# First pair of chunks: invert 16x16 blocks only and finish by block substitution on TensorE

## The chip, the cores and the metric

The kernel runs on one core of a Trainium2 chip. The metric is the device time of one execution in microseconds; the time before is the median of three runs, and one more execution was profiled. The engines are called as in the profile: PE is TensorE, PEld its weight loads, DVE is VectorE, ACT is ScalarE, POOL is GpSimd, SP is SyncE, which issues most DMAs.

## What is computed

Three layers follow each other; the change lies in the first.

```python
# 1: delta-rule attention, 32 heads (4 x 8), 768 steps, head size 48
k_n = k / (norm(k) + 1e-6)
for t in range(768):
    y[t] = q[t] @ state
    v_old = state.T @ k_n[t]
    state += beta[t] * outer(k_n[t], v[t] - v_old)
# 2: soft mixture of 8 experts, weights P from 8 Sinkhorn rounds over x @ w_gate
out = sum_e P[:, e] * (relu(x @ w1[e]) @ w2[e])
# 3: ((x @ w1) * (x @ w2)) @ w3 @ w_out
```

The 768 steps are cut into 12 chunks of 64. Inside a chunk the steps are solved together: with G the Gram matrix of the chunk's keys, L its strict lower triangle with rows scaled by beta, a chunk needs u = inverse(I + L) times (scaled v minus what the old state predicts). From u follow the chunk's output and the new state.

## The kernel before, in words

**Layout.** A chunk holds 32 heads x 64 steps: 128 partitions are two groups of 64 steps, and 16 heads lie side by side in each. Two chunks make a pair (j = 0 to 5). A "quad group" below is the helper `quads`: 32 small matmuls in float32, four at a time in the four 64x64 tiles of the array. The trace shows each float32 matmul as two records, so a quad group is 64 records.

**A pair's preparation.** `prep_k` loads keys, squares and sums them (ACT, DVE), takes Sqrt on ACT and a Newton step on DVE (`newton`), computes the Gram matrices (PE, "b<-kt") and copies them out of PSUM into `a` and `g`. `invert` then inverts all the 32x32 diagonal blocks of a pair together on DVE: a transposition, 7 small product-and-sum steps for 8x8 blocks, products of 512 elements for 16x16 blocks, products of 1024 elements for 32x32 blocks, and two transpositions (L602, L604). `tt_make` joins two 32x32 inverses to a 64x64 one by PE matmuls of 32x32 ("b<-asys,g" and "b<-tt,g") and copies; the result is `tt`. `prep_q` computes the masked products of queries and keys (`pt`).

**A chunk's recurrence.** `seq(c)`: the old state predicts v ("b<-st,kt"), DVE subtracts, PE multiplies by the inverse ("b<-vs,tt"), two ACT copies give `u`, "b<-u,kraw" the state (copied to `st` on ACT) and "b<-pt,u" the output. The output is copied to `xst` (ACT), goes to DRAM and comes back in another layout (the DMAs xs_d<-xst and xst<-xs_d), and is split by ACT and POOL or DVE into the high and low part `xr`.

**The first expert beside it.** `e0(c)` computes expert 0 for the 256 tokens of a chunk: 144 matmuls with 128x128 weights and 256 columns ("b<-xr,wA" and "b<-hA,wA"). It needs the chunk's `xr` and has the lowest priority, so PE fills its gaps with it. The router's logits are "b<-xr,wg" and "b<-masks,yr". After chunk 11 come the Sinkhorn rounds ("b<-cs,ones"), then the other experts and the third layer.

**What sets the order.** Everything is recorded as operations with priorities; a planner in the program (`Plan.order`) places them by its own cost figures and writes each engine's list before anything runs. On the chip each engine follows its list in order, and waits at the head of it.

Two columns of the small input `masks` (64 and 65) hold -1 for the first and for the second 32 steps of 64; with them ACT and DVE copy the two 32x32 diagonal blocks of a Gram matrix into `a`.

Of the kernel before, what the change touches and what calls it, by code (L numbers as in the profile page):

```python
# [6 lines left out]
F32 = mybir.dt.float32  # L7
# [11 lines left out]
NG = 16  # L19
D = 48  # L20
# [290 lines left out]
def act(n, psum=False):  # L311
    return (n / 1.2 + (110 if psum else 150)) / 1000
# [22 lines left out]
class Kernel:  # L335
# [56 lines left out]
    def setup(self):  # L392
        nc, T, g = self.nc, self.T, self.g
        n = NCH * NG
        self.open("const", "left", ones=((128, 128), F32), masks=((128, 75), F32),
                  wgr=((128, 3, NE), F32), p=((128, NTT + 1, NE + 1), F32),
# [24 lines left out]
        self.bank = [pp.tile([128, 512], F32, tag=f"b{i}", name=f"b{i}") for i in range(8)]  # L421
        self.psum = Ring(range(8), caps={"attn": 4, "eh": 1, "ey": 1, "hx": 6, "yb": 2, "h": 4, "y": 4})
        a = self.a
# [35 lines left out]
    def prep_k(self, c):  # L459
# [8 lines left out]
        sq = lambda: T["kn"][:, kn.at]  # L468
        g.op({"ACT": act(768)}, lambda e: nc.scalar.activation(out=sq(), in_=sq(), func=AF.Square), r=[], w=[kn], prio=pr)
        nr = lambda i: T["nrm"][:, i]  # L470
        g.op({"DVE": dve(768) + .07}, lambda e: nc.vector.tensor_reduce(out=nr(0)[:, 16 * st:16 * st + 16], in_=sq(), axis=AX.X, op=ALU.add),  # L471
             r=[kn], w=[("n0", st)], prio=pr)
        if st:
            n0 = [("n0", 0), ("n0", 1)]
            bm = lambda: T["bm"][:, 32 * j:32 * j + 32]
            nv = lambda: T["nv"][:, 32 * j:32 * j + 32]
            g.op({"DVE": .1}, lambda e: nc.vector.tensor_scalar(out=nr(0), in0=nr(0), scalar1=1e-30, scalar2=None, op0=ALU.max), w=n0, prio=pr)
            g.op({"ACT": .15}, lambda e: nc.scalar.activation(out=nr(1), in_=nr(0), func=AF.Sqrt), r=n0, w=["n1"], prio=pr)
# [10 lines left out]
            g.op({"DVE": 1.3}, newton, r=n0 + ["bm"], w=["n1", ("bm", j), ("nv", j)], prio=pr)  # L489
        gi = j % NG12  # L490
        pg = pr if j == 0 else -120.0 + j
# [7 lines left out]
        g.op({"PE": 8 * QUAD}, gram, ins=128, r=[k], w=sg + [(self.a0[j], "z")] + [  # L499
            (n, gi, st, hf) for n in ("g12", "xsb0", "xsb1") for hf in range(2)], prio=pg)  # L500
        for hf in range(2):
            gs = slice(8 * hf, 8 * hf + 8)
            s = sg[hf]
            ss = slice(16 * st + 8 * hf, 16 * st + 8 * hf + 8)
            a0 = self.a0[j]
            ak = (a0, st, hf)
            g.op({"ACT": act(256, True)}, lambda e, s=s, ss=ss, a0=a0: self.copy(
                "ACT", T["a0"][:, a0.at, ss], self.ps(s, 8, 64)[:, :, 0:32], T["masks"][:, 64:65]), r=[s, "masks"], w=[ak], prio=pg)
            g.op({"ACT": act(256, True)}, lambda e, s=s, gs=gs, st=st: self.copy(
                "ACT", T["g12"][:, gi, st, gs], self.ps(s, 8, 64)[:, :, 32:64], -1.0),  # L510
                r=[s], w=[(n, gi, st, hf) for n in ("g12", "xsb0", "xsb1")], prio=pg)
            g.op({"DVE": dve(256)}, lambda e, s=s, ss=ss, a0=a0: self.stt(
                T["a0"][:, a0.at, ss], self.ps(s, 8, 64)[:, :, 32:64], T["masks"][:, 65:66], T["a0"][:, a0.at, ss], ALU.mult, ALU.add),
                r=[s, "masks", ("g12", gi, st, hf)], w=[ak], prio=pg)

# [15 lines left out]
    def invert(self, j):  # L531
# [75 lines left out]
    def tt_make(self, c):  # L607

        nc, g, T = self.nc, self.g, self.T
        st = c % 2  # L610
        pr = 10.0 * (c // 2) + 2 + st
        a0 = self.a0[c // 2]
        gi = c // 2 % NG12
        tt = self.TT[c] = self.ttring.new()
        bk = ("bm", c // 2)
        for hf in range(2):
            gs = slice(8 * hf, 8 * hf + 8)
# [36 lines left out]
            for b in range(2):  # L654
# [3 lines left out]
                    r=[s2, bk], w=[tk(1 + b)], prio=pr)  # L658

    def prep_q(self, c):  # L660

        nc, g, T = self.nc, self.g, self.T
        pr = 10.0 * (c // 2) + 2.5 + c % 2
        pd = pr if c > 1 else 4.0
        q = self.Q[c] = self.qring.new()
        self.dma(lambda: T["qt"][:, q.at].rearrange("p g t -> p (g t)"), lambda: self.a["qT"][c], 524288, [], [q], pr - 20)
        k = self.K[c]
        sp = [self.psum.new("attn") for _ in range(2)]
        for hf in range(2):
# [6 lines left out]
        for hf in range(2):  # L676
            s, pt = sp[hf], self.PT[c, hf]
            g.op({"DVE": dve(512)}, lambda e, s=s, pt=pt, hf=hf: self.tt(
                e, T["pt"][:, pt.at // 2, pt.at % 2], self.ps(s, 8, 64),
                T["masks"][:, 0:64].rearrange("p (o t) -> p o t", o=1).to_broadcast([128, 8, 64]), ALU.mult), r=[s, "masks"], w=[pt], prio=pr)  # L680

# [10 lines left out]
    def seq(self, c):  # L692
        nc, g, T = self.nc, self.g, self.T
        pr = -100.0 + c
        m = len(g.ops)
# [4 lines left out]
        self.dma(lambda: va().rearrange("p g d -> p (g d)"), lambda: self.vsrc(c), 393216, [], vk, 10.0 * j - 16.9 if j else -16.0 + c)  # L700
        g.op({"POOL": 1.5, "DVE": dve(768) + .08}, lambda e: self.tt(
            e, va(), va(), T["nv"][:, 16 * c:16 * c + 16].rearrange("p (s o) -> p s o", o=1).to_broadcast([128, NG, D]), ALU.mult),
            r=[("nv", j)], w=vk, prio=10.0 * j + .5)
        kr = self.kraw.new()
# [29 lines left out]

        def um(e):
# [3 lines left out]
        for hf in range(2):  # L739
            g.op({"ACT": act(384, True)}, lambda e, hf=hf: self.copy("ACT", T["u"][:, u.at, 8 * hf:8 * hf + 8], self.ps(su[hf], 8, D)),  # L740
                 r=[su[hf]], w=[(u, hf)], prio=pr)
        uk = [(u, 0), (u, 1)]
        if c < NCH - 1:
            if c == 0:
# [697 lines left out]
def layouts(inputs):  # L1442
# [50 lines left out]
```

## Time and profile before

| what | us |
|---|---|
| median of 3 runs | 2096.46 |
| lowest and highest of them | 2087.47, 2102.5 |
| the profiled execution | 2087.25 |
| its span | 2085.4 |
| PE busy in the span | 2021.4 |
| DVE busy | 1236.4 |
| ACT busy | 709.9 |

The profiled execution took 1.85 us more than its span, what lies around the first and last instruction. The busy share of PE is an average of stages: the first 50 us and the rest are not alike, so the stages are read one by one. Matmul ends are modelled and overlap, so the pace of PE is read from the start of one group to the start of the next.

### The profile page before, as it was taken

To read this page: it belongs to the slowest core of one execution; us is meant where nothing else is said; L and a number is where in the kernel's file an instruction comes from. 1 tells how busy PE (TensorE), PEld (TensorE's weight loads), DVE (VectorE), ACT (ScalarE), POOL (GpSimd) and SP (SyncE) were. 2 spreads that over 40 slices of the span, in tenths; PEclk is the share of its full clock that TensorE was granted. 3 is DMA by queue.
4 is the path that set the end of the run, shared out by engine and by line. 5 is a ranking of instruction groups with operands and counts; after the bars stand their busy time and mean duration, and the time that the engine had idled before them with its cause. 6 is when DMAs were issued, how large, how long until landed. Compare 5 with 4: busy or idle time off the path is not lost.

```text
span 2085.4 us, 39076 instructions
## 1 busy us (share of the span) xinstructions
PE 2021.4 (97%) x16017; PEld 1732.8 (83%) x16017; DVE 1236.4 (59%) x1970; ACT 709.9 (34%) x1355; POOL 804.4 (39%) x856
## 2 busy tenths in 40 slices
PE   1899999999999999999999999999999999999999
PEld 1899889988888888888888888788888888988888
DVE  7998884585444445866666677776667643222222
ACT  2544333344434434423323324233333322222222
POOL 3111101056767667444554453444554534200000
PEclk9999999999999999999999999999999999999999
DMA  6523333276445456755646545656556537410000
GB/s 220 160 88 104 106 91 109 81 257 238 180 182 215 178 187 232 250 183 214 236 162 211 192 143 203 229 203 210 190 176 214 192 107 206 97 36 16 16 21 25
DMA packets 166611, 331.58 MB, mean 159 GB/s; under 512 B 13408, under 2 KB 117792, under 8 KB 154912
## 3 DMA queue, kind: packets, MB, share of 16 engines
q1 hardware_dynamic: 132544, 193.82, 27.5%
q0 software_dynamic: 33888, 135.28, 19.1%
q8 instruction: 125, 2.05, 0.4%
q14 instruction: 54, 0.44, 0.1%
HBM read 235.10 MB, written 93.95 MB: 158 GB/s over the span
## 4 chain that ended last, share of the span: by engine, by line
PE 88%; DVE 4%; issue 4%; DMA 2%; POOL 1%; ACT 0%; SPq 0%; POOLq 0%; DVEq 0%; ACTq 0%
PE b L357 88%; DMA acc<-y_d 1%; DVE prod L368 1%; DMA kt<-in_kT 1%; DVE t L568 0%; DMA rawB<-in_moe_w 0%; POOL wA L368 0%; SPq L388 0%; DVE xs L568 0%; POOL sums L368 0%; DVE asys L602 0%; DVE asys L542 0%; DVE nrm L471 0%; DVE cv L368 0%; DVE cv L371 0%
## 5 line engine op out<-in xcount | busy, mean ns | idle before, releaser
L357 PE MATMUL b<-hA,wA 128*128 128x512 f32 (+1 forms) x2367 | 504.7, 353 | 2.5 <-DVE hA L371 2.5
L357 PEld LDWEIGHTS b<-hA,wA 128*128 128x128 f32 x2367 | 391.1, 189 | 64.7 <-DVE hA L371 3.3
L368 POOL TENSOR_TENSOR acc<-acc,tmp 128x512 f32<-128x512 f32 x252 | 335.9, 1335 | 196.8 <-DVE tmp L368 194.5
L357 PE MATMUL b<-hB,wA 128*128 128x512 f32 x1521 | 386.1, 389 | 0.0
L357 PEld LDWEIGHTS b<-hB,wA 128*128 128x128 f32 x1521 | 285.6, 188 | 59.1
L357 PE MATMUL b<-xr,wA 128*128 128x256 f32 (+1 forms) x1620 | 328.9, 337 | 0.0
L357 PEld LDWEIGHTS b<-xr,wA 128*128 128x128 f32 x1620 | 251.5, 190 | 32.4
L361 ACT ACTIVATE rt<-b 128x512 f32<-128x512 f32 x300 | 178.8, 597 | 249.6 <-PE b L357 244.0
L357 PE MATMUL b<-xT,wA 128*128 128x512 f32 x1008 | 249.8, 389 | 1.2 <-POOL wA L368 1.2
L368 DVE TENSOR_TENSOR b<-b,rt 128x512 f32<-128x512 f32 x252 | 173.3, 694 | 103.4 <-ACT rt L361 75.7
L357 PEld LDWEIGHTS b<-xT,wA 128*128 128x128 f32 x1008 | 189.1, 188 | 41.0 <-POOL wA L368 2.0
L368 POOL TENSOR_TENSOR cv<-cv 128x256 f32<-128x256 f32 (+3 forms) x179 | 131.7, 736 | 204.7 <-DVE cv L1255 112.3
L357 PE MATMUL b<-xT,wS 128*128 128x512 f32 x756 | 199.0, 389 | 0.8 <-ACT rt L361 0.8
L368 DVE TENSOR_TENSOR tmp<-b,pb 128x512 f32<-128x512 f32 x150 | 103.3, 690 | 138.5 <-PE b L357 134.3
L371 DVE SCALAR_TENSOR_TENSOR hA<-b,hA 128x512 fp32r<-128x512 f32 x215 | 143.9, 687 | 63.1 <-ACT hA L1060 37.3
L357 PEld LDWEIGHTS b<-xT,wS 128*128 128x128 f32 x756 | 141.9, 188 | 30.6 <-ACT rt L361 1.2
L368 DVE TENSOR_TENSOR rt<-b,rt 128x512 f32<-128x512 f32 x48 | 33.2, 692 | 186.0 <-PE b L357 186.0
L368 DVE TENSOR_TENSOR tmp<-b,yr 128x512 f32<-128x512 f32 x102 | 70.3, 690 | 111.2 <-PE b L357 103.3
L371 DVE SCALAR_TENSOR_TENSOR hB<-b,hB 128x512 fp32r<-128x512 f32 x169 | 115.2, 684 | 24.5 <-ACT hB L1060 24.2
L1060 ACT ACTIVATE hB<-b 128x512 fp32r<-128x512 f32 x169 | 100.6, 596 | 80.7 <-DVE b L368 78.2
L368 POOL TENSOR_TENSOR wA<-rawB,wA 128x768 fp32r<-128x768 f32 (+1 forms) x54 | 92.4, 1723 | 85.7 <-ACT wA L361 85.0
L361 ACT ACTIVATE cv<-cv 128x256 fp32r<-128x256 f32 x72 | 29.1, 404 | 265.2 <-DVE cv L371 265.2
(171 smaller groups left out, 2394.8 us busy)
## 6 DMA issues: line engine op xcount, KB each, us to landing
wA<-wq_d POOLq DMA_DIRECT2D x56, 1536.0 KB, 8.6
wq_d<-wA SPq DMA_DIRECT2D x28, 1536.0 KB, 7.3
wS<-ws_d POOLq DMA_DIRECT2D x56, 512.0 KB, 4.8
rawB<-in_moe_w SPq DMA_DIRECT2D x108, 192.0 KB, 3.1
ws_d<-wS SPq DMA_DIRECT2D x28, 512.0 KB, 4.2
w_d<-cv SPq DMA_DIRECT2D x112, 128.0 KB, 1.8
cvr<-in_w3T SPq DMA_DIRECT2D x32, 256.0 KB, 2.7
wS<-w_d POOLq DMA_DIRECT2D x32, 256.0 KB, 3.5
```

The costliest lines, as they stand in the source:

```text
L357: self.nc.tensor.matmul(*args, skip_group_check=True, **kw)
L361: self.nc.scalar.activation(out=out, in_=in_, func=AF.Copy, **({} if scale is None else {"scale": scale}))
L368: self.E[eng].tensor_tensor(out=out, in0=in0, in1=in1, op=op)
L371: self.nc.vector.scalar_tensor_tensor(out=out, in0=in0, scalar=scalar, in1=in1, op0=op0, op1=op1)
L1060: g.op({"ACT": actb(512)}, lambda e: nc.scalar.activation(out=hv(0), in_=self.ps(s, 512), func=AF.Relu), r=[s], w=[(out, 0, 0)], prio=pe)
```

## The change

For the first pair (chunks 0 and 1) `invert` stops after the 16x16 blocks: one transposition instead of two, and the six products and sums of 1024 elements are not made. `tt_make` for these chunks multiplies the block inverses by beta (DVE, two operations of 512), lets one quad group multiply them with the part of the Gram matrix below the 16x16 diagonal blocks, and copies the result into 128x128 block-diagonal matrices R (two heads in each, 8 for each half of a chunk; `rb` gives their place in `xst`, `g12` and a new tile `gm`). The R matrices are first zeroed by POOL and filled with 16-column strips of the negated, masked Gram matrix by ACT (12 strips for each chunk). In `seq`, what "b<-vs,tt" gives is now the start value; u comes from three rounds of u = start + R u, each round 2 halves of 8 full 128x128 float32 matmuls with 48 columns and one DVE addition per half.

Around it: a Sqrt on one element at the start loads ACT's table early; v of the first two chunks is scaled on ACT, 32 copies of 48 columns, instead of on POOL; the Gram copies of all chunks are done by ACT alone, with strips of 32 partitions, in place of two DVE operations; priorities of the first chunks and of the third and fourth Gram matrices are raised. The pairs 1 to 5 keep their inversion.

```diff
+        g.op({"ACT": 1.5}, lambda e: nc.scalar.activation(out=T["nrm"][:, 1, 0:1], in_=T["ones"][:, 0:1], func=AF.Sqrt), r=["ones"], w=["n1"], prio=-30)
...
+        if j == 0:
+            g.op({"DVE": 2.05}, lambda e: nc.vector.transpose(
+                out=av().rearrange("p s i -> p i s"), in_=tm().rearrange("p c i -> p i c")),
+                r=["t", ("t8", 0), ("t8", 1), ("tr", 0), ("tr", 1)], w=ka, prio=pr + .1)
...
+            return
...
+        if c < 2:
...
+            g.op({"PE": 8 * QUAD}, lambda e: self.quads([self.ps(s, 8, 64) for s in sr],
+                 lambda r, x, y, m: self.rb(c, x)[r, m, 64 * y:64 * y + 64], lambda r, x, y, m: T["tt"][r, tt.at, x, m],
+                 lambda x, y: (y, x ^ y, y)), ins=128, r=rk + [(tt, hf, i) for hf in range(2) for i in range(3)], w=sr, prio=pr)
...
+        if c < 2:
+            for hf in range(2):
+                g.op({"ACT": act(384, True), "DVE": dve(384)}, lambda e, hf=hf, su=su: self.copy(e, V(hf), self.ps(su[hf], 8, D)),
+                     r=[su[hf]], w=[(v, hf)], prio=pr)
+            for it in range(3):
+                su = two()
+                for hf in range(2):
+                    def rv(e, it=it, s=su[hf], hf=hf):
+                        for m in range(8):
+                            self.mm(self.ps(s, 8, D)[:, m], self.rb(c, hf)[:, m], (T["u"][:, u.at] if it else T["vs"][:, v.at])[:, 8 * hf + m], start=True, stop=True)
+                    uh = [(u, hf)]
+                    g.op({"PE": 8 * .1}, rv, ins=32, r=[("R", c, hf, 0), ("R", c, hf, 1)] + self.rbk(c, hf) + (uh if it else [(v, hf)]), w=[su[hf]], prio=pr)
+                    g.op({"DVE": dve(384)}, lambda e, hf=hf, su=su: self.tt(e, T["u"][:, u.at, 8 * hf:8 * hf + 8], self.ps(su[hf], 8, D), V(hf), ALU.add),
+                         r=[su[hf], (v, hf)], w=uh, prio=pr)
```

DVE, the end of the first inversion (asys, t, prod, xs and a are its tiles, pt and tt what follows). Before:

```order
L368 TENSOR_TENSOR prod<-a_113,xs 128x1024
L568 TENSOR_REDUCE t<-prod 128x8x16
L368 TENSOR_TENSOR pt<-b_138,masks 128x512
L602 STREAM_TRANSPOSE asys<-t 128x32x32
L604 STREAM_TRANSPOSE a_113<-t 128x32x32
L368 TENSOR_TENSOR pt<-b_139,masks 128x512
L368 TENSOR_TENSOR tt<-a_113,bm 128x8x32 x2
```

The same place now, where L580 is the sum that was L568:

```order
L368 TENSOR_TENSOR prod<-a_113,xs 128x512 x2
L580 TENSOR_REDUCE t<-prod 128x8x8 x2
L600 STREAM_TRANSPOSE a_113<-t 128x32x32
L368 TENSOR_TENSOR tt<-a_113,bm_118 128x16x32 x2
L368 TENSOR_TENSOR pt<-b_140,masks 128x512
L368 TENSOR_TENSOR pt<-b_141,masks 128x512
L368 TENSOR_TENSOR tt<-a_113,bm_118 128x16x32 x2
```

The 1024-element products and one transposition are gone, and `tt` follows the remaining transposition at once.

PE, from the last matmul of chunk 1's "b<-vs,tt" to the first matmuls of e0(0). Before:

```order
L357 MATMUL b_134<-vs,tt 64x48
L357 MATMUL b_139<-xr,wA 128x256 x3
L357 MATMUL b_140<-xr,wg 16x256 x3
L357 MATMUL b_140<-xr,wg 8x256 x3
L357 MATMUL b_139<-xr,wA 128x256 x9
```

Now (g_112 and gm hold the R matrices of chunk 1's two halves):

```order
L357 MATMUL b_143<-vs,tt 64x48
L357 MATMUL b_136<-vs,g_112 128x48 x8
L357 MATMUL b_138<-vs,gm 128x48 x8
L357 MATMUL b_142<-xr,wA 128x256 x3
L357 MATMUL b_143<-u,g_112 128x48 x8
L357 MATMUL b_136<-u,gm 128x48 x8
L357 MATMUL b_138<-xr,wg 16x256 x3
L357 MATMUL b_138<-xr,wg 8x256 x3
L357 MATMUL b_143<-u,g_112 128x48 x8
L357 MATMUL b_136<-u,gm 128x48 x8
L357 MATMUL b_142<-xr,wA 128x256 x6
```

The three rounds of chunk 1 stand among the first matmuls of e0(0).

ACT, around the first `xr`, chunk 0's output that came back from DRAM. Before:

```order
L361 ACTIVATE xr<-xst 128x768
L469 ACTIVATE kn<-kn 128x768
L478 ACTIVATE nrm<-nrm 128x32
L469 ACTIVATE kn<-kn 128x768
L361 ACTIVATE u<-b_138 128x384
L361 ACTIVATE u<-b_134 128x384
```

Now:

```order
L471 ACTIVATE kn<-kn 128x768 x2
L361 ACTIVATE xr<-xst 128x768
L361 ACTIVATE vs<-b_142 128x384
L361 ACTIVATE vs<-b_143 128x384
L361 ACTIVATE wA<-yr 128x768
```

In both lists chunk 1's copies out of PSUM stand behind `xr`; they gave `u`, and now give the start value `vs` of the three rounds.

From the Sinkhorn rounds on, PE's list is the same in both kernels.

## Rows read from the trace of the kernel before

**Rows 1.** Busy time by stage: length, PE, PEld, DVE, ACT, POOL, granted clock, DMA, GB/s.

```profile
0.00:50.00 50.00, 7.94 (x256) 7.20 (x256) 38.64 (x55) 14.66 (x24) 16.58 (x18) 1.00 0.63 223
50.00:85.00 35.00, 27.95 (x897) 26.12 (x898) 33.99 (x74) 19.30 (x42) 6.44 (x5) 1.00 0.52 159
...
100.00:390.00 290.00, 285.01 (x6784) 263.19 (x6782) 220.05 (x333) 109.20 (x251) 31.61 (x31) 1.00 0.35 105
...
430.00:2085.00 1655.00, 1646.26 (x7433) 1383.76 (x7432) 897.75 (x1414) 544.39 (x993) 747.26 (x801) 1.00 0.49 170
```

**Rows 2.** Waits of PE in the first 100 us: total, times, longest.

```profile
PE b L357 <- DVE asys L602: 34.4, 1, 34.4
PE b L357 <- DVE vs L371: 3.8, 1, 3.8
```

**Rows 3.** Timeline of DVE, 10 to 56 us: start, busy, instruction.

```profile
13.92 0.35 DVE L482 RECIPROCAL nrm<-nrm 128x32 f32<-128x32 f32 x1 [1.06 <-ACT nrm L478]
...
16.58 1.40 DVE L488 TENSOR_TENSOR bm<-bm,nrm 128x32 f32<-128x32 f32 x1
17.90 1.89 DVE L542 STREAM_TRANSPOSE asys<-a 128x1024 f32<-128x1024 f32 x1
...
30.12 0.69 DVE L568 TENSOR_REDUCE t<-prod 128x64 f32<-128x512 f32 x1
30.85 1.23 DVE L368 TENSOR_TENSOR prod<-asys,t 128x1024 f32<-128x1024 f32 x1
...
50.15 1.99 DVE L604 STREAM_TRANSPOSE a<-t 128x1024 f32<-128x1024 f32 x1
52.00 0.67 DVE L368 TENSOR_TENSOR pt<-b,masks 128x512 f32<-128x512 f32 x1
```

**Rows 4.** Timeline of ACT, three stretches of the first 140 us.

```profile
12.36 1.28 ACT L478 ACT_TABLE_LOAD   x1
...
30.73 0.83 ACT L361 ACTIVATE wA<-yr 128x768 fp32r<-128x768 f32 x1
...
67.16 0.87 ACT L361 ACTIVATE u<-b 128x384 f32<-128x384 f32 x2 [0.83 <-PE b L357]
...
70.24 1.06 ACT L361 ACTIVATE xst<-b 128x512 f32<-128x512 f32 x2
81.34 0.84 ACT L361 ACTIVATE xr<-xst 128x768 fp32r<-128x768 f32 x1 [0.90 <-DMA xst<-xs_d]
...
130.79 1.09 ACT L361 ACTIVATE xst<-b 128x512 f32<-128x512 f32 x2 [1.61 <-PE b L357]
138.91 0.84 ACT L361 ACTIVATE xr<-xst 128x768 fp32r<-128x768 f32 x1 [0.76 <-DMA xst<-xs_d]
```

**Rows 5.** Timeline of PE, 48 to 200 us: matmul groups, x is their records.

```profile
55.15 4.02 PE L357 MATMUL b<-kt 48*64 48x64 f32 x128
...
65.15 1.96 PE L357 MATMUL b<-vs,tt 64*64 64x48 f32 x64
...
86.80 1.89 PE L357 MATMUL b<-xr,wA 128*128 128x256 f32 x9
88.62 1.16 PE L357 MATMUL b<-kt 48*64 48x64 f32 x64
...
90.62 0.94 PE L357 MATMUL b<-u,kraw 64*48 64x48 f32 x64
91.48 0.61 PE L357 MATMUL b<-masks,yr 16*128 16x8 f32 x4
92.02 2.05 PE L357 MATMUL b<-xr,wA 128*128 128x256 f32 x15
...
126.13 1.15 PE L357 MATMUL b<-vs,tt 64*64 64x48 f32 x64
```

**Rows 6.** Timeline of PE's weight loads near 395 us: a float32 load of 128 columns.

```profile
395.04 0.31 PEld L357 LDWEIGHTS b<-cs,ones 128*128 128x128 f32 x2
395.28 0.66 PEld L357 LDWEIGHTS b<-xr,wA 128*128 128x128 f32 x5
```

More of the change, by code (lines that the diff above doesn't have):

```diff
@@ L394, in setup @@
         n = NCH * NG
-        self.open("const", "left", ones=((128, 128), F32), masks=((128, 75), F32),
+        self.open("const", "left", ones=((128, 128), F32), masks=((128, 78), F32),
                   wgr=((128, 3, NE), F32), p=((128, NTT + 1, NE + 1), F32),
@@ L421, in setup @@
         self.bank = [pp.tile([128, 512], F32, tag=f"b{i}", name=f"b{i}") for i in range(8)]
-        self.psum = Ring(range(8), caps={"attn": 4, "eh": 1, "ey": 1, "hx": 6, "yb": 2, "h": 4, "y": 4})
+        self.psum = Ring(range(8), caps={"attn": 4, "early": 2, "eh": 1, "ey": 1, "hx": 6, "yb": 2, "h": 4, "y": 4})
         a = self.a
@@ L453, in setup @@
         self.SX = None
+        self.XB = [self.yring.new() for _ in range(2)]
     def vsrc(self, c):
@@ L477, in prep_k @@
             g.op({"DVE": .1}, lambda e: nc.vector.tensor_scalar(out=nr(0), in0=nr(0), scalar1=1e-30, scalar2=None, op0=ALU.max), w=n0, prio=pr)
-            g.op({"ACT": .15}, lambda e: nc.scalar.activation(out=nr(1), in_=nr(0), func=AF.Sqrt), r=n0, w=["n1"], prio=pr)
+            g.op({"ACT": .25}, lambda e: nc.scalar.activation(out=nr(1), in_=nr(0), func=AF.Sqrt), r=n0, w=["n1"], prio=pr)
             def newton(e):
@@ L488, in newton @@
                 v.tensor_tensor(out=bm(), in0=bm(), in1=nr(2), op=ALU.mult)
[L489 removed]
+            g.op({"DVE": 1.9}, newton, r=n0 + ["bm"], w=["n1", ("bm", j), ("nv", j)], prio=pr)
         gi = j % NG12
[L491 removed]
+        pg = pr if j == 0 else -120.0 + j if j > 1 else -99.5
         if st == 0:
             self.a0[j] = self.aring.new()
+        if j == 0:
+            for hf in range(2):
+                g.op({"POOL": 1.0}, lambda e, hf=hf: nc.gpsimd.memset(self.rb(c, hf), 0.0), w=self.rbk(c, hf), prio=-6 + c)
         sg = [self.psum.new("attn") for _ in range(2)]
@@ L506, in prep_k @@
             ak = (a0, st, hf)
+            if j:
+                g.op({"ACT": act(256, True)}, lambda e, s=s, gs=gs, st=st: self.copy(
+                    "ACT", T["g12"][:, gi, st, gs], self.ps(s, 8, 64)[:, :, 32:64], -1.0),
+                    r=[s], w=[(n, gi, st, hf) for n in ("g12", "xsb0", "xsb1")], prio=pg)
             g.op({"ACT": act(256, True)}, lambda e, s=s, ss=ss, a0=a0: self.copy(
[L508 to L514, printed above, removed]
+                "ACT", T["a0"][:, a0.at, ss], self.ps(s, 8, 64)[:, :, 0:32], -1.0), r=[s], w=[ak], prio=pg)
+            for r in (slice(32, 64), slice(96, 128)):
+                g.op({"ACT": act(256, True)}, lambda e, s=s, ss=ss, a0=a0, r=r: self.copy(
+                    "ACT", T["a0"][r, a0.at, ss], self.ps(s, 8, 64)[r, :, 32:64], -1.0), r=[s], w=[ak], prio=pg)
+            for h in range(2) if j == 0 else ():
+                for i in range(3):
+                    r = slice(64 * h, 64 * h + 64)
+                    g.op({"ACT": act(128, True)}, lambda e, s=s, hf=hf, i=i, r=r, h=h: self.copy(
+                        "ACT", self.rb(c, hf)[r, :, 64 * h + 16 * i:64 * h + 16 * i + 16], self.ps(s, 8, 64)[r, :, 16 * i:16 * i + 16],
+                        T["masks"][r, 75 + i:76 + i]), r=[s, "masks"], w=self.rbk(c, hf), prio=pg + 1.3 + c)
     TDONE = [("t16", 1, 0), ("t16", 1, 8), ("t16", 0)]
@@ L586, in invert @@
                  lambda p=p: xt(p, 8), 8, 8, 8, [("tr", p), ("x8", p)], [("t8", p)])
+        if j == 0:
+            g.op({"DVE": 2.05}, lambda e: nc.vector.transpose(
+                out=av().rearrange("p s i -> p i s"), in_=tm().rearrange("p c i -> p i c")),
+                r=["t", ("t8", 0), ("t8", 1), ("tr", 0), ("tr", 1)], w=ka, prio=pr + .1)
+            for i in range(2):
+                g.op({"ACT": .18}, lambda e, i=i: self.copy("ACT", T["bm2"][:, i], T["bm"][:, 0:32], T["masks"][:, (74, 64)[i]:(75, 65)[i]]),
+                     r=[("bm", 0), "masks"], w=[("bm2", i)], prio=pr)
+            return
         rk = ["asys", "t", ("t8", 0), ("t8", 1)]
@@ L615, in tt_make @@
         bk = ("bm", c // 2)
+        if c < 2:
+            view = lambda nm, at: T[nm][:, at].rearrange("p h (m t) -> p h m t", t=64) if nm == "xst" else T[nm][:, at]
+            for i in range(2):
+                g.op({"DVE": dve(512)}, lambda e, i=i: self.tt(
+                    e, T["tt"][:, tt.at].rearrange("p h m t -> p (h m) t")[:, :, 32 * i:32 * i + 32], T["a0"][:, a0.at, 16 * st:16 * st + 16],
+                    T["bm2"][:, i, 16 * st:16 * st + 16].rearrange("p (s o) -> p s o", o=1).to_broadcast([128, 16, 32]), ALU.mult),
+                    r=[(a0, st, 0), (a0, st, 1), ("bm2", i)], w=[(tt, hf, 2 * i) for hf in range(2)] + ([(tt, hf, 1) for hf in range(2)] if i else []), prio=pr)
+            sr = [self.psum.new("attn") for _ in range(2)]
+            rk = self.rbk(c, 0) + self.rbk(c, 1)
+            g.op({"PE": 8 * QUAD}, lambda e: self.quads([self.ps(s, 8, 64) for s in sr],
+                 lambda r, x, y, m: self.rb(c, x)[r, m, 64 * y:64 * y + 64], lambda r, x, y, m: T["tt"][r, tt.at, x, m],
+                 lambda x, y: (y, x ^ y, y)), ins=128, r=rk + [(tt, hf, i) for hf in range(2) for i in range(3)], w=sr, prio=pr)
+            for hf in range(2):
+                for h in range(2):
+                    g.op({"ACT": act(512, True), "DVE": dve(512)}, lambda e, hf=hf, h=h: self.copy(
+                        e, self.rb(c, hf)[64 * h:64 * h + 64, :, 64 * h:64 * h + 64], self.ps(sr[hf], 8, 64)[64 * h:64 * h + 64]),
+                        r=[sr[hf]] + self.rbk(c, hf), w=[("R", c, hf, h)], prio=pr)
+            return
         for hf in range(2):
@@ L658, in tt_make, with rb, rbk @@
                     r=[s2, bk], w=[tk(1 + b)], prio=pr)
+    def rb(self, c, hf):
+        v = self.T["gm"] if c and hf else self.T["g12"][:, 0].rearrange("p a s i -> p (a s i)") if c else self.T["xst"][:, hf].rearrange("p h t -> p (h t)")
+        return v.rearrange("p (m t) -> p m t", t=128)
+    def rbk(self, c, hf):
+        return ["gm"] if c and hf else [(n, 0, a, b) for n in ("g12", "xsb0", "xsb1") for a in range(2) for b in range(2)] if c else [(self.XB[hf], "gm")]
     def prep_q(self, c):
         nc, g, T = self.nc, self.g, self.T
-        pr = 10.0 * (c // 2) + 2.5 + c % 2
+        pr = 10.0 * (c // 2) + 2.5 + c % 2 if c else -129.0
         pd = pr if c > 1 else 4.0
         q = self.Q[c] = self.qring.new()
-        self.dma(lambda: T["qt"][:, q.at].rearrange("p g t -> p (g t)"), lambda: self.a["qT"][c], 524288, [], [q], pr - 20)
+        self.dma(lambda: T["qt"][:, q.at].rearrange("p g t -> p (g t)"), lambda: self.a["qT"][c], 524288, [], [q], (pr if c else 2.5) - 20)
         k = self.K[c]
-        sp = [self.psum.new("attn") for _ in range(2)]
+        sp = [self.psum.new("attn" if c > 1 else "early") for _ in range(2)]
         for hf in range(2):
@@ L700, in seq, with scale @@
         self.dma(lambda: va().rearrange("p g d -> p (g d)"), lambda: self.vsrc(c), 393216, [], vk, 10.0 * j - 16.9 if j else -16.0 + c)
-        g.op({"POOL": 1.5, "DVE": dve(768) + .08}, lambda e: self.tt(
-            e, va(), va(), T["nv"][:, 16 * c:16 * c + 16].rearrange("p (s o) -> p s o", o=1).to_broadcast([128, NG, D]), ALU.mult),
-            r=[("nv", j)], w=vk, prio=10.0 * j + .5)
+        for i in range(4) if j == 0 else ():
+            def scale(e, i=i):
+                for x in range(4 * i, 4 * i + 4):
+                    self.copy("ACT", va()[:, x], va()[:, x], T["nv"][:, 16 * c + x:16 * c + x + 1])
+            g.op({"ACT": .8}, scale, r=[("nv", 0)], w=[vk[i // 2]], prio=1.2 + c)
+        if j:
+            g.op({"POOL": 1.5, "DVE": dve(768) + .08}, lambda e: self.tt(
+                e, va(), va(), T["nv"][:, 16 * c:16 * c + 16].rearrange("p (s o) -> p s o", o=1).to_broadcast([128, NG, D]), ALU.mult),
+                r=[("nv", j)], w=vk, prio=10.0 * j + .5)
         kr = self.kraw.new()
@@ L738, in seq @@
         g.op({"PE": 8 * QUAD}, um, ins=128, r=vk + [(tt, hf, i) for hf in range(2) for i in range(3)] + [("qs", c)], w=su, prio=pr)
-        for hf in range(2):
-            g.op({"ACT": act(384, True)}, lambda e, hf=hf: self.copy("ACT", T["u"][:, u.at, 8 * hf:8 * hf + 8], self.ps(su[hf], 8, D)),
-                 r=[su[hf]], w=[(u, hf)], prio=pr)
         uk = [(u, 0), (u, 1)]
+        if c < 2:
+            for hf in range(2):
+                g.op({"ACT": act(384, True), "DVE": dve(384)}, lambda e, hf=hf, su=su: self.copy(e, V(hf), self.ps(su[hf], 8, D)),
+                     r=[su[hf]], w=[(v, hf)], prio=pr)
+            for it in range(3):
+                su = two()
+                for hf in range(2):
+                    def rv(e, it=it, s=su[hf], hf=hf):
[5 more added lines that the diff above has]
+                         r=[su[hf], (v, hf)], w=uh, prio=pr)
+        else:
+            for hf in range(2):
+                g.op({"ACT": act(384, True)}, lambda e, hf=hf: self.copy("ACT", T["u"][:, u.at, 8 * hf:8 * hf + 8], self.ps(su[hf], 8, D)),
+                     r=[su[hf]], w=[(u, hf)], prio=pr)
         if c < NCH - 1:
@@ L1460, in layouts @@
     t = np.arange(64)
-    masks = np.zeros((128, 75), np.float32)
+    masks = np.zeros((128, 78), np.float32)
     masks[:, :64] = i[:, None] < t[None, :]
-    masks[:, 64] = -1.0 * (i < 32)
-    masks[:, 65] = -1.0 * (i >= 32)
     masks[:, 74] = i < 32
+    masks[:, 64] = i >= 32
+    for b in range(3):
+        masks[:, 75 + b] = -1.0 * (i >= 16 * b + 16)
     masks[:, 66:74] = i[:, None] % NE == t[None, :NE]
```

18 lines of the change are left out of this document (9 added, 9 removed).

## The prediction

> **What bounds the kernel now.** I read the busy time by stage first. PE works 7.94 of the first 50 us, 27.95 of the next 35, and then 285.01 of 290 and 1646.26 of 1655 [rows 1]: from about 85 us on PE has no room, and it has filler for every gap, the matmuls of e0. From the Sinkhorn rounds on its list is the same in both kernels. So the change is worth what it does to the moment at which PE becomes full, less the PE work that it leaves behind that moment. The waits come next: of the first 100 us PE spends 34.4 in one wait for DVE's L602, the end of the first inversion [rows 2]. DVE's timeline shows what stands there: Sqrt's result at 13.92, the inversion from 17.90, the 16x16 blocks done at 30.81 (30.12 + 0.69), then 1024-element steps and two transpositions until 52.14 [rows 3].
>
> Last, PE's pace. The granted clock reads 1.00 in every stage [rows 1], yet the same 64 records "b<-vs,tt" took 1.96 us at 65.15 and 1.15 at 126.13 [rows 5]. Nine e0 matmuls took 1.89 at 86.80, fifteen took 2.05 at 92.02: about 0.2 us for 256 columns, then about 0.13. The two paces fit the levels 1.2 and 2.4 GHz, so I take the records' pace and not the column. It rose between 86.80 and 88.62, after the first 256-column matmuls; small-tile groups such as the 4.02 us of "b<-kt" at 55.15 had not raised it [rows 5]. Before e0 starts I price PE at the slow pace.
>
> **The change part by part, as moments in chunk 0.**
>
> 1. Start. The table load of 1.28 us goes from between the key norms and Sqrt [rows 4]. The two beta products on DVE took 1.18 and 1.40 while POOL scaled v at their side; with v on ACT they cost what their neighbours of 128x32 cost, 0.2 each. From 13.92 the Newton step lasted until 17.98 (16.58 + 1.40) [rows 3]; now I have it from 12.5 until 14.4. Gain 3.6.
>
> 2. Inversion. 17.90 to 30.81 is 12.9 us and stays, so 14.4 becomes 27.3. ACT delays it: between Sqrt and the two copies of `t` its list now has 28 copies of 48 columns, the strips for R and Gram copies. From 0.53 us for 512 and 0.43 for 384 columns [rows 4] a 48-column copy is about 0.17, an estimate; the two copies come about 1.2 late. That gives 28.5. Then 21.3 us of DVE work (30.81 to 52.14) goes, one transposition of 1.99 stays [rows 3]: 30.5. Every chunk also loses two DVE operations for ACT strips; ACT is busy 109.20 of 290 us [rows 1], which hides them, and without that cover they would cost about 1 us a chunk.
>
> 3. Building R. Two DVE products of 512 at 0.67 [rows 3], a quad group at 1.96 [rows 5]: 33.9. Four ACT copies at 0.53, one weight copy of 0.83 that stands in between, two start-value copies, 0.87 together [rows 4]: 37.9, with hand-overs 38.1. The zeroing on POOL and "b<-vs,tt" lie beside this, and so do the Gram groups of chunks 2 and 3, moved ahead on PE, 4 us at the slow pace while PE would wait for DVE; without that cover they would come on top. SP's loads ahead of them keep their order, and the early Sqrt ends long before the first keys are squared.
>
> 4. The three rounds, which no row shows. A round's half is 8 full-array float32 matmuls, 16 records. Above: the 128-column float32 loads at 395.04 start 0.12 us apart (395.04, then twice until 395.28) [rows 6], and four records "b<-masks,yr" with such loads last from 91.48 to 92.02, 0.135 each [rows 5]. At this, the fast pace, a half is 1.9 to 2.1 us; at the slow pace, times 1.8, it is 3.5 to 3.7. Below: 64 records "b<-u,kraw" took 0.94 for 48x48 tiles [rows 5]; four tiles make one array, so 16 records would be at least 0.94 fast, 1.7 slow. I take 3.5, because the load of 128 columns is the nearest row and the pace before e0 is slow: for 64-column weights both paces are in the rows, and the load is not spared (1.96 against 1.15 with only 48 columns streaming). Six halves are 21.0, the quad group "b<-qt,kt" among them 2.0, the last addition with its hand-overs 0.8 (512 elements are 0.67 [rows 3]): u of chunk 0 at 61.9. Before it was there at 68.03 (67.16 + 0.87) [rows 4]. Gain so far 6.1.
>
> **Chunk 1, where it is given back.** Two quad groups (state, output) after 61.9 give 66.0, two copies of 0.53 `xst` at 67.3. The way through DRAM took 10.0 us the first time (71.30 to 81.34) and 7.0 at a later chunk (131.88 to 138.91) [rows 4]; with 8.5, ACT starts `xr` at 75.8 and ends it at 76.7. Chunk 1's start-value copies stand behind `xr` on ACT's list. Their matmuls are done by then (three quad groups and a subtraction after 66.0, about 73), so PE waits some 4 us for a DMA that it does not need. Copies until 77.6; round one 7.0; three e0 matmuls 0.8 at 85.4; round two 7.0; logits 1.3; round three 7.0: 100.7. Behind these on SP and POOL nothing is late, since the weights' loads end before. Before, PE had done the same work (start of the nine e0 matmuls, 86.8 with their load just ahead) at 86.6 [rows 5], and one Gram and one query group more, 2.2 us. So PE is full 16.3 us later. Some comes back: with more e0 in hand PE loses less of the 5.0 us that it idles between 100 and 390 [rows 1]; I take half, 2.5. Sum: 14 us slower.
>
> The profiled execution took 2087.25, so the sum stands at about 2101; its 9.2 us distance to the median of 2096.46 is the spread of runs, which no edit changes. I forecast 2096.46 + 14, 2110 us. That is 0.7%, inside the 1% that a measurement of this kernel tells from no change.
>
> The rule that speaks on step 4 is in the Trainium skill, "TensorE: Matmul & The Clock Gate", section "LDWEIGHTS (loading the stationary operand)": a load costs its columns over 1.2 GHz, 107 ns for 128, with no word of the pace. At the fast pace the trace agrees (0.12); at the slow pace it does not (64-column groups, 1.96 against 1.15). By it a half would be 1.7 us at either pace; what that makes of the time is the second rival.
>
> **Rivals.**
>
> *PE is at the fast pace in the rounds: faster.* The rounds keep the whole array at work for a long stretch, which no group before 85 us does. For: the pace does rise when full-array matmuls come, at 86.80 to 88.62. Against: those streamed 256 columns, the rounds stream 48, and PE ran without a long break from 55 to 70 at the slow pace [rows 5]. Then a half is 1.95, a quad group 1.1: rounds from 37.2, u at 50.8, `xst` at 54.2, `xr` done at 63.5, chunk 1's copies at 64.4, round one until 68.3, three e0 and logits 1.2, two rounds 7.8: 77.3, with the 2.2 us 79.5, against 86.6. That is 7 faster, 2089. It decides this way as soon as a half costs under about 2.3 us.
>
> *The load costs 0.12 us at the slow pace too: a little faster.* Streaming 48 columns would hide behind it, a half 1.9. With slow quad groups u is at 52.4, `xr` done at 67.0, copies 67.9, three rounds, e0 and logits until 81.4, with 2.2 us 83.6: 3 faster, 2093. Against it stands the 64-column pair of rows. The Trainium skill's rule above is this mechanism.
>
> *Chunk 2 starves PE: slower still.* DVE's additions of chunk 1 stand in its list among the products of the second inversion, so these wait for the slow rounds too; what is left of them (about 16 us by rows 3) and `tt_make` then puts chunk 2's `xr` near 142. PE holds 36 us of e0 and some 16 of small groups for the 42 us from 100.7, so it should not run dry; if it does, by 8 us, the time is 2118 to 2120.
>
> **How the numbers follow.** Slow rounds 0.63, fast pace 0.16, load at one price 0.09, chunk 2 starving 0.10, something faster still (rounds at the lower bound, 0.94 a half: u at 44.7, 19 faster) 0.02. The likeliest alone reaches from 2098 to 2122: a half of 3.1 to 3.7 (12 halves, 5 us and 3 us) and a way through DRAM of 7 to 10, with a few us of spread. Down to the first two rivals the range becomes 2086 to 2122. Slower by over 1% (2117.4) needs the starving case or the upper end of the likeliest: 0.19. Faster by over 1% (2075.5) is left to the lower bound: 0.03. The rest is within 1%: 0.78.
>
> **What would show it.** Right: a matmul "b<-vs,xst" or "b<-u,xst" group of 16 records near 3.5 us; the first `tt` product near 30.5; u near 62; chunk 1's `vs` copies on ACT directly behind `xr`; the first e0 matmuls near 85 and PE full from about 101. Wrong: a group under 2.3 us, or e0 in full flow before 85.

## The result, and the profile after

The changed kernel takes 2123.99 us (median of 4 runs, 2121.95 to 2126.46); the kernel before, beside it, 2094.28. The ratio is 1.0141, 95% interval 1.0101 to 1.0180: 30 us slower, by over 1%. The forecast was 14 us slower, 0.7%. The profiled execution of after has a span of 2122.1 us.

Busy time by stage of the changed kernel answers to [rows 1], with its columns:

```profile
0.00:50.00 50.00, 25.47 (x567) 24.19 (x568) 30.93 (x58) 38.81 (x109) 11.84 (x18) 0.93 0.60 214
50.00:85.00 35.00, 29.66 (x468) 28.56 (x468) 24.54 (x40) 8.49 (x15) 13.82 (x8) 0.50 0.44 133
...
100.00:390.00 290.00, 277.14 (x6935) 253.78 (x6935) 219.13 (x337) 121.86 (x286) 33.00 (x34) 0.95 0.35 104
465.00:2120.00 1655.00, 1647.21 (x7436) 1383.58 (x7434) 895.23 (x1414) 544.47 (x993) 747.66 (x801) 1.00 0.50 169
```

The last 1655 us are as before. From 100 to 390 us PE is idle for 12.9 us where it was idle for 5.0, and the granted clock is 0.95 on average, not 1.00. The loss has two parts. The nine e0 matmuls start at 101.86 instead of 86.80 [rows 5]: 15.1 us. ACT's first "xr<-xT" comes at 459.97 instead of 424.67; from it to the end of the span it is 1662.1 and 1660.7 us, so hardly anything more is lost behind it. Before, and in the changed kernel:

```profile
424.67 0.62 ACT L361 ACTIVATE xr<-xT 128x512 fp32r<-128x512 f32 x1
```

```profile
459.97 0.62 ACT L361 ACTIVATE xr<-xT 128x512 fp32r<-128x512 f32 x1
```

So some 20 us more went between 100 and 460 in this pair of profiles.

DVE's timeline (start, busy, instruction) answers to [rows 3], ACT's last two lines to [rows 4], PE's to [rows 5]:

```profile
14.11 0.19 DVE L490 TENSOR_TENSOR bm<-bm,nrm 128x32 f32<-128x32 f32 x1
14.22 1.91 DVE L554 STREAM_TRANSPOSE asys<-a 128x1024 f32<-128x1024 f32 x1
...
27.75 1.29 DVE L368 TENSOR_TENSOR prod<-a,xs 128x512 f32<-128x512 f32 x2 [3.13 <-ACT a L361]
...
30.39 2.01 DVE L600 STREAM_TRANSPOSE a<-t 128x1024 f32<-128x1024 f32 x1
```

```profile
74.86 0.84 ACT L361 ACTIVATE xr<-xst 128x768 fp32r<-128x768 f32 x1 [2.99 <-DMA xst<-xs_d]
75.61 0.85 ACT L361 ACTIVATE vs<-b 128x384 f32<-128x384 f32 x2
```

```profile
21.66 1.97 PE L357 MATMUL b<-kt 48*64 48x64 f32 x60 [1.30 <-ACT xst L361]
...
40.53 4.76 PE L357 MATMUL b<-vs,xst 128*128 128x48 f32 x32 [1.04 <-ACT vs L361]
45.10 7.03 PE L357 MATMUL b<-u,xst 128*128 128x48 f32 x32
...
53.97 7.06 PE L357 MATMUL b<-u,xst 128*128 128x48 f32 x32
...
76.13 3.65 PE L357 MATMUL b<-vs,g 128*128 128x48 f32 x16 [2.77 <-ACT vs L361]
...
95.02 3.61 PE L357 MATMUL b<-u,gm 128*128 128x48 f32 x16
...
101.86 1.33 PE L357 MATMUL b<-xr,wA 128*128 128x256 f32 x9
```

The front runs as it was worked out: 16 records of a half in 3.5 to 3.65 us, u of chunk 0 at 61.6 (its last addition starts at 61.07), chunk 1's start-value copies directly behind `xr` while PE waits 2.77. Only the first round is quicker, 4.76 for two halves. Stretches of the trace of after show why, and where the clock is low later (length, the engines as above, granted clock):

```profile
40.00:43.00 3.00, 2.46 (x22) 2.47 (x23) 0.81 (x2) 2.98 (x6) 2.95 (x2) 1.00 0.25 91
43.00:45.00 2.00, 2.00 (x12) 2.00 (x11) 0.45 (x1) 0.39 (x2) 0.63 (x1) 0.52 0.73 225
45.00:100.00 55.00, 49.66 (x565) 47.95 (x564) 34.26 (x54) 10.55 (x18) 16.92 (x9) 0.50 0.30 91
...
238.00:252.00 14.00, 11.40 (x176) 9.90 (x172) 11.22 (x27) 3.38 (x10) 2.59 (x2) 0.63 0.06 20
252.00:335.00 83.00, 79.16 (x2184) 73.11 (x2176) 74.96 (x106) 32.51 (x74) 9.40 (x8) 1.00 0.36 107
335.00:350.00 15.00, 14.64 (x202) 13.19 (x202) 4.37 (x9) 4.67 (x11) 1.86 (x3) 0.55 0.00 1
```

At 40 to 43 us a round's record takes 2.46 / 22 = 0.11 us at the full clock (2.4 GHz); at 0.50 (1.2 GHz), 3.61 / 16 = 0.23. The rounds run nearly all at the lower level. The two low stretches behind 200 us come with PE waits for `hA`, the hidden values of the expert, which PE reads next. At 238 us the rows of DVE, POOL and PE are these:

```profile
237.70 1.50 DVE L489 TENSOR_TENSOR bm<-bm,nrm 128x32 f32<-128x32 f32 x1
239.24 1.40 DVE L490 TENSOR_TENSOR bm<-bm,nrm 128x32 f32<-128x32 f32 x1
240.67 0.69 DVE L371 SCALAR_TENSOR_TENSOR hA<-b,hA 128x512 fp32r<-128x512 f32 x1
```

```profile
237.35 1.81 POOL L368 TENSOR_TENSOR xr<-xst,xr 128x768 fp32r<-128x768 f32 x1 [9.93 <-ACT xr L361]
239.12 1.47 POOL L368 TENSOR_TENSOR vs<-vs,nv 128x768 f32<-128x768 f32 x1
```

```profile
241.41 0.58 PE L357 MATMUL b<-hA,wA 128*128 128x256 f32 x1 [2.60 <-DVE hA L371]
```

The beta products of pair 4 (`bm`, beta over the key norms, L489 and L490) stand ahead of `hA` in DVE's list and take 1.4 to 1.5 us while POOL works, 0.19 at the start. The second low stretch has another wait: PE waits 1.75 us until 335.36, and there `hA` stands behind the inversion's two transpositions (L622 and L624, 330.87 to 334.58), not behind beta products.

That beta products stand at 238 us has its cause in the squares of the keys. Before, and in the changed kernel (operation, count, least, median and most ns, first and last start):

```profile
L469 ACT ACTIVATE kn<-kn x12: 827/843/845, 5.9 to 88.5; 128x768 f32<-128x768 f32 x12
```

```profile
L471 ACT ACTIVATE kn<-kn x12: 826/840/853, 6.6 to 259.9; 128x768 f32<-128x768 f32 x12
```

The diff lets the squares of pairs 2 to 5 wait for `t8`, the 8x8 products, of the pair ahead. The description of the change above does not name this operand, nor a second one of its kind; both stand with the run that leaves them out. All squares were done by 90 us and the last beta products by 130; now each pair's squares come just in time, at 70, 151, 204 and 258 us, and the last beta products at 292, amid the `hA` work.

### The profile page after: what moved, and what is told of

It reads as the page before. It is cut to its first block, busy times and chain, and to the rows that moved or that the text cites. A ratio compares the mean times of both kernels' runs of the same rounds, so it can differ in the third digit from the quotient of the medians.

```text
span 2122.1 us, 39237 instructions
## 1 busy us (share of the span) xinstructions
PE 2068.7 (97%) x16081; PEld 1777.6 (84%) x16081; DVE 1214.5 (57%) x1940; ACT 736.8 (35%) x1447; POOL 807.0 (38%) x860
## 4 chain that ended last, share of the span: by engine, by line
PE 90%; DMA 4%; DVE 2%; ACT 2%; issue 1%; POOL 1%; SPq 0%; DVEq 0%; ACTq 0%; POOLq 0%
PE b L357 90%; DMA acc<-y_d 1%; DMA xs_d<-xst 1%; DMA xst<-xs_d 1%; DMA rawB<-in_moe_w 0%; POOL wA L368 0%; ACT vs L361 0%; DMA kn<-in_kn 0%; DMA kt<-in_kT 0%; ACT xst L361 0%; ACT a L361 0%; SPq L388 0%; ACT g L361 0%; DVE hA L371 0%; DVE tmp L368 0%
```

## Experiments

A, B and C are the theories of each expectation. Code is shortened: "..." stands for what is left out, X for `vs` in the first round and `u` in the others.

**The rounds.** All on the changed kernel. The first has one matrix for eight (the other seven are left out, so u is not the reference's), with the lists unchanged:

```diff
-for m in range(8):
-    self.mm(self.ps(s, 8, D)[:, m], self.rb(c, hf)[:, m], X[:, 8 * hf + m], ...)
+self.mm(self.ps(s, 8 * D), self.rb(c, hf)[:, 0], X[:, 8 * hf:8 * hf + 8] as 384 columns, ...)
```

> Leaves out 7 of the 8 R matrices of each half: one matmul with the first of them and all 384 columns stands for the 8 matmuls of 48 columns, so u of chunks 0 and 1 is not the reference's; every engine's list is otherwise that of the changed kernel, word for word. Theory A (the loss is the rounds' duration, and the late stage loses because its list was planned for short rounds): a half costs about 0.7 us at the fast pace or 1.3 at the slow one instead of 3.5, PE is full near 75 us instead of 98, the granted clock does not fall after 100 us, total 2075 to 2090. Theory B (the late loss comes from other parts of the change, above all the Gram copies on ACT): PE is full near 75 us too, but the waits and falls of the clock after 100 us stay, total 2097 to 2107.

2095.02, ratio 0.9993 (0.9982 to 1.0004): between the two, 5 us past A's end and 2 short of B's start. Cheap rounds take 29 us away. Two halves with as many streamed columns as before, but an eighth of the loads, take 1.65 us, with the clock at 0.92:

```profile
42.84 1.65 PE L357 MATMUL b<-u,xst 128*128 128x384 f32 x4
```

But the nine e0 matmuls start at 76.83, 10 us earlier than before, and the median is that of the kernel before: something else in the change eats those 10 us. The waits are B's (PE idles 12.8 us from 100 to 350), the clock is A's (0.97 or more there).

The same product as two tiles, so that the zero blocks are not loaded:

```diff
 for m in range(8):
-    self.mm(self.ps(s, 8, D)[:, m], self.rb(c, hf)[:, m], X[:, 8 * hf + m], ...)
+    for h in range(2):
+        r = slice(64 * h, 64 * h + 64)
+        self.mm(self.ps(s, 8, D)[r, m], self.rb(c, hf)[r, m, r], X[r, 8 * hf + m], ..., tile_position=(64 * h, 64 * h))
```

> R holds two 64x64 blocks on its diagonal and zeros beside them; here each of its matmuls is made as two of 64x64 in two tiles of the array, the lists of the other engines stay. Theory A: the price of a half goes with the columns of a weight load and two tiles run at a time, so a half is about 1.75 us at the slow pace (0.027 us a record for four tiles, twice that for two, 32 records) and 1.1 at the fast one; PE full near 80 us, total 2085 to 2098. If a half goes with the number of records or with full-array use, it stays at 3.5 or grows to 7, and the total is 2124 or more. Theory B: 2105 to 2112.

2092.96, ratio 0.9985 (0.9962 to 1.0008): A. Its groups on PE, two halves at the full clock, then one half at the lower one:

```profile
40.16 2.07 PE L357 MATMUL b<-vs,xst 64*64 64x48 f32 x64 [1.11 <-ACT vs L361]
```

```profile
65.58 1.91 PE L357 MATMUL b<-vs,gm 64*64 64x48 f32 x32
```

A half costs 1.0 and 1.9 us in place of 1.8 and 3.6. With the run before (0.8 a half, the same 384 streamed columns) that shows the weight load of 128 columns as what a half pays for.

The planner's price of a half, 0.8 us, set to what it took (`{"PE": 8 * .1}` to `{"PE": 3.5}`):

> One figure of the planner is changed, the price of a round's half, from 0.8 to 3.5 us; the same work in another order. Theory A: the rounds still last 3.5 us a half and PE is full near 98 us, but the list after it fits, so of the 21 us lost between 100 and 460 us most come back: 2103 to 2112. Theory B: what is lost after 100 us stays, 2118 to 2128.

2121.12, ratio 1.0114 (1.0092 to 1.0137): B. The wrong price is not the cause; put right, it brings back 3 us. With the tiles, and their price of 1.75:

> The changed kernel with each product of a round as two 64x64 tiles, and with the planner told that a half of a round takes 1.75 us in place of 0.8 (measured there: 1.75 at the lower clock, 1.0 at the full one). Theory A (the lists only shuffle where TensorE's short waits fall, a few us either way): 2088 to 2100 us. Theory B (a plan with the right price keeps the front's gain of 7 us that the tiles brought): 2084 to 2088 us.

2094.78, ratio 0.9996 (0.9980 to 1.0012): A.

The one-matrix kernel with its product written four times (`for _ in range(4):`), so that the duration returns without the loads:

> The changed kernel with one R matrix in place of eight (it leaves out seven of eight, and a round is one product of 384 columns), and that product written four times over: the lists of every engine are those of the changed kernel, a half of a round takes about as long as there (4 x 0.8 us at the full clock, more at half), but with a quarter of the weight loads. With the product written once this kernel took 2095.02 us. Theory A (the rounds cost their duration: a late front with these lists pays twice): 2116 to 2128 us, with the product xr by wA in groups of 9 at 99 to 104 us. Theory B (half of the loss is due to the weight loads: they leave the clock at its lower level at 100 us, and the late stage starts from there): 2104 to 2113 us at the same moment of that product.

2119.33, ratio 1.0121 (1.0090 to 1.0152): A, though the nine e0 matmuls start at 97.59, 1.4 us before A's stretch, and the clock is at full from 87 to 100 us:

```profile
87.00:100.00 13.00, 13.00 (x179) 9.19 (x177) 8.29 (x10) 2.03 (x5) 0.00 (x0) 1.00 0.19 58
```

So it is not the clock level at 100 us that the late loss comes from, but a late front with these lists.

**Lateness and the lists.** First, a second profile of each kernel, unchanged.

> The kernel before, unchanged, for one more profiled execution. The profile read for the prediction was one of 2087.25 us, while the runs beside the changed kernel have a median near 2095 us. Theory A (the lateness of the front is paid for again between 100 and 460 us, by short PE waits each followed by a stretch at the lower clock): a typical execution of before keeps PE busy there as in the first profile; its stage of the first feed-forward product starts (ACT xr<-xT) at 424 to 428 us, and the granted clock is 0.97 or more from 100 to 400 us. Theory B (the first profile was a lucky one, and before loses there too): that stage starts at 431 to 440 us, with a clock under 0.95 in some 50 us between 100 and 400.

2099.51; "xr<-xT" at 433.58, clock 0.86 from 250 to 300 us. B: in this execution the kernel before loses 9 us there, and in the one behind the prediction it did not.

> The changed kernel once more, for a second profiled execution beside one of 2122.1 us. In the first, from 87 us to the row xr<-xT (460.0 us) PE's work, counted as records by their duration at the full clock, leaves some 42 us over; in three executions of before and its close relatives 20, 33 and 36 us. Theory A (the loss after 100 us belongs to these lists and this lateness, not to one execution): xr<-xT at 456 to 463 us, a granted clock below 0.95 in at least two of the stretches of 50 us between 100 and 400. Theory B (chance of one execution): xr<-xT at or under 452 us.

2119.40; "xr<-xT" at 454.01, below A's bounds and above B's; clock 0.93 in three of the stretches. The hole is the same: PE waits 2.61 us for `hA` until 242.18. The second wait is there too, 1.71 us until 336.46, but the clock stays at 1.00 from 335 to 350. The late loss belongs to the lists, in part; some 6 us of it belonged to the execution.

The kernel before with nothing but a late front:

```diff
 def um(e):
-    self.quads(...)
+    for _ in range((8, 4)[c] if c < 2 else 1):
+        self.quads(...)
```

> Before, with the product u = T v of chunk 0 written 8 times into the same bank and that of chunk 1 4 times (10 more groups of 64 records of TensorE, nothing else): the front alone is late, by 10 groups of 1.96 us at the slow pace (19.6 us) or less where the clock rises meanwhile (1.06 us each, 10.6 us). Every other engine's list stays. Theory A (lateness by itself costs about twice over, since DVE, which is 44 of 50 us busy from 100 to 300 us, and TensorE then meet differently and TensorE's waits lower its clock): 2113 to 2130 us. Theory B (lateness carries one to one, and the second half of the loss comes from something else in the change): the shift of the product xr by wA in groups of 9 (86.8 us in before) less at most 2, so 2103 to 2110 us at a shift of 10 to 14 us. Theory C (it is recovered in the later stage): under 2101 us.

2110.16, ratio 1.0066 (1.0041 to 1.0091); nine e0 matmuls at 100.83, 14.0 later, time 14.5 longer (9 to 19 by the interval): B. With the lists of before lateness costs about itself.

The changed kernel without its two orderings:

```diff
-r=[("t8", 0)] if j > 1 else [], w=[kn]
+r=[], w=[kn]
-r=[k] + ([("pu", 0)] if j == 2 else [])
+r=[k]
```

> The changed kernel without its two added orderings: the squares of later chunks no longer wait for the inverse's product t8, and the Gram product of pair 2 no longer waits for chunk 0's pu. Theory A (the rounds' duration is the loss): 2118 to 2130 us. Theory B (the orderings hold back pairs 1 and 2, and the late loss of 14 us is theirs): 2108 to 2113 us, with xr<-xT at or under 450 us.

2110.45, ratio 1.0070 (1.0046 to 1.0093): B. The front is as late as before this edit (the group "b<-xr,wA x6" at 99.49, 98.42 with the orderings), "xr<-xT" at 444.52. Leaving out the Gram ordering alone gives the same lists as the changed kernel, so all of it is the ordering of the squares.

What it costs is seen in PE's idle time and clock. From 100 to 425 us PE idles 12.9 us in the changed kernel, 10.8 in its second profile and 7.1 here; the low clock takes 16.0, 10.5 and 3.5 (an estimate: over stretches of 50 us, length times what the granted clock lacks to 1.00). Together that is 28.9, 21.3 and 10.6, and the way from the group "b<-xr,wA x6" to "xr<-xT" is 361.6, 354.6 and 345.0. The waits for `hA` are only a part of it: 4.3 us in two waits in the changed kernel, 3.2 in four here. The squares now end at 130 us, and the beta products of pair 4 are back at their own price:

```profile
L471 ACT ACTIVATE kn<-kn x12: 826/842/848, 6.6 to 130.2; 128x768 f32<-128x768 f32 x12
```

```profile
130.61 0.19 DVE L489 TENSOR_TENSOR bm<-bm,nrm 128x32 f32<-128x32 f32 x1
130.84 0.19 DVE L490 TENSOR_TENSOR bm<-bm,nrm 128x32 f32<-128x32 f32 x1
```

The ordering alone, put into the kernel before:

```diff
-r=[], w=[kn]
+r=[("t8", 0)] if j > 1 else [], w=[kn]
```

> Before with one edit of the change alone: the squares of the keys of pairs 2 to 5 wait for the 8x8 products (t8) of the pair ahead. In the changed kernel that puts the squares at 70, 151, 204 and 258 us, one pair at a time, where before has them all done by 89 us; without it the changed kernel took 2110.45. Theory A (this ordering is the second half of the loss: the norms and beta products come just in time, among DVE's hA, and TensorE waits there): 2102 to 2112 us, with DVE's bm products spread to beyond 200 us. Theory B (it costs only together with the late front or the other lists): 2092 to 2100 us.

2100.41, ratio 1.0031 (1.0014 to 1.0048): between the two, at B's edge. Alone it costs about 5 us. The beta products spread as A said (one at 221.68 takes 1.24 us), but PE's waits from 100 to 430 are not for `hA`: 5.6 us have no releaser in the profile and 3.3 are for the keys' DMA. Here the cost takes another path.

**Other parts.** The ACT-only Gram copies in the kernel before (a DVE multiply-add goes, two ACT strips come):

> The kernel before with one part of the change: the Gram copies of all chunks by ACT alone, in strips of 32 partitions, in place of two DVE operations. Theory A: within 5 us of the kernel before, 2089 to 2099, clock at 1.00 after 100 us. Theory B: 10 to 21 us slower, 2104 to 2115, with waits of PE for DVE hA and falls of the clock after 100 us.

2099.46, ratio 1.0019 (1.0001 to 1.0036): some 4 us, just past A's end. The opposite edit, the old copies for pairs 1 to 5 in the tiled kernel:

> The changed kernel with each product of a round as two 64x64 tiles (so that the zero blocks are not loaded), and with the Gram copies of before (an ACT mask copy and a DVE multiply-add) for all pairs but the first. Theory A (the rounds' duration is the loss, and the ACT copies of the later pairs cost some 4 us by themselves, as the copies alone did in before): 2085 to 2091 us. Theory B (the copies' cost is within the noise of where waits fall): 2091 to 2098 us.

2099.15, ratio 1.0018 (1.0000 to 1.0036), 6 us more than the tiles alone, and the two intervals touch: both theories missed. Either direction costs some us, so no price of the copies can be read from these two; both edits also reorder everything behind them.

The early table and v scaled on ACT, in the kernel before:

> Before with two edits of the change alone: the Sqrt table loaded early, and v of chunks 0 and 1 scaled on ACT in place of POOL. Theory A (the start gain of 3.6 us exists, but a front that is earlier by a few us is not kept between 100 and 425 us): 2089 to 2097 us. Theory B (it carries one to one): 2088 to 2092 us, with the ACT row xr<-xT 3 to 4 us earlier than in before.

2093.01, ratio 0.9988 (0.9973 to 1.0003): within A, 1 us past B's end. The nine e0 matmuls start 4.0 us earlier (82.84), but "xr<-xT" is at 427.26, later than in the first profile of before and earlier than in the second; the time is 2.6 us less, not distinct from none.

**Both causes undone:** the two tiles, and no ordering of the squares.

> The changed kernel with each product of a round as two 64x64 tiles and without the ordering of the squares behind t8. Theory A (two causes, each undone: the rounds' weight loads of 128 columns, 14 us, and the ordering of the squares, 4 us or more with an early front): 2081 to 2089 us. Theory B (the ordering matters only where the front is late): 2089 to 2096 us.

2086.95, ratio 0.9966 (0.9953 to 0.9978): A by the median. It beats both kernels: 8 us under the one before, 37 under the changed one. Its long middle has the clock at 0.99 where after had 0.95 (100 to 420 us), and the squares end at 107 us:

```profile
100.00:420.00 320.00, 312.81 (x6946) 290.89 (x6944) 225.70 (x378) 127.47 (x291) 32.20 (x34) 0.99 0.31 95
```

## Why the prediction was wrong

Right in direction and in the front, it went wrong on what lies behind.

- *Start:* bm was to be done at 14.4 and was at 14.30.
- *Inversion:* the transposition was to end at 30.5 and ended at 32.40. ACT's 28 small copies held its two copies of `t` by more than the 1.2 us given, a copy of 48 columns taking 0.23 to 0.25, not 0.17: DVE waited 3.13.
- *Building R:* rounds from 40.53, not 38.1; 1.9 of it is the step ahead.
- *Rounds:* a half of 3.5 was right, at the price of the 128-column load at the lower clock. The first rival (full clock) held for about 3 us, which made up the 2.4: u at 61.6, forecast 61.9. The second rival, the rule of "LDWEIGHTS (loading the stationary operand)" in the Trainium skill, "TensorE: Matmul & The Clock Gate" (columns over 1.2 GHz, with no word of the level), agrees at the full clock, 0.11 us a record at 1.00, and fails at the lower one, 0.23 at 0.50.
- *Chunk 1:* `xr` at 74.86 (75.8), copies behind it as said, round three done at 98.6 (100.7). By the prediction's reckoning, against 86.6 less 2.2, PE is full 14.2 us later; forecast 16.3.
- *"Some comes back … I take half, 2.5":* this is the step that failed. The sum lets the lists behind 100 us give something back and has no term for what they lose. The run with a late front and the lists of before shows about nothing either way (14.5 us of time for 14.0 of lateness, too coarse to tell 2.5 from none). In the changed kernel another 13.5 us (2123.99 less 2110.45) go, 9 by its second execution (2119.40), and the run without the ordering of the squares shows where: in that one operand of the diff, for which my part-by-part sum had no term. It takes the squares out of the gap before 90 us and puts them among `hA`; PE then waits more and runs longer at the lower clock. The forecast, 2110, is what the change costs without it; that it is met so closely is in part luck, since a front 2 us less late than forecast makes up for the 2.5 that should have come back.
- *The rival "chunk 2 starves PE"* had nearly the size, 2118 to 2120, and not the mechanism: PE does not run dry for 8 us. It idles 12.9 us in short waits between 100 and 390, and in the first profile its clock stood at the lower level for a while at the longest ones (0.63 from 238 to 252, 0.55 from 335 to 350); in the second only at the longer of the two.

Open stays by which waits the ordering costs its time, beyond the one at 238 us; why it costs 5 us in the kernel before, some 6 in the tiled one (2092.96 to 2086.95, not clear of the noise) and 9 to 13.5 with the late front; and what the Gram copies cost by themselves. Each edit replans all lists, and where PE's short waits fall moves by some us with it.

## What to carry to other kernels

Price every changed dependency of a diff, also one that names no new work: follow where it moves the operation in its engine's list, and what stands behind it there. Here a matmul that streams 48 columns cost its weight load; ask whether zero blocks can stay unloaded, by cutting it into tiles. And take two profiles of a kernel whose stage has short waits before trusting that it idles for only 5 us.

## What the runs showed of the hardware

- The clock fell while PE had no break: from 1.00 to 0.50 within the rounds of the changed kernel, from 43 us on, with PE busy since 40.53. In the run with the price of 3.5 it fell again behind 256-column matmuls, 0.86 from 90 to 93 us, 0.70 to 96, then 0.50 for 14 us of rounds, with PE busy throughout. In the run with the product written four times it stayed at 1.00 from 81 to 100 us, over all but the start of chunk 1's rounds with their 384 columns.
- The column of the granted clock reads 1.00 over the first 40 us of after, yet there 60 records "b<-kt" take 1.97 us; 64 of them take 1.16 at 103.11. Over that stretch the records' pace is the better witness.
- A 128x32 product on DVE took 0.19 us alone and 1.4 to 1.5 beside POOL's 768-element products.
